# The first routing's clearings and its lists, and the places of VectorE's side work in two mixture networks, moved on one Trainium2 core

## The chip, the cores and the metric

The kernel runs on one core of one Trainium2 chip. The metric is device microseconds (us) of one execution, the median of three runs. A core has four compute engines with instruction queues of their own, TensorE (PE; its weight loads are shown apart, as PEld), VectorE (DVE), ScalarE (ACT) and GpSimd (POOL); each works through its queue in order and waits where an operand isn't there. SyncE (SP) issues most of the DMA transfers, also in order.

## The reference

```python
x = np.fft.fft(np.fft.fft(x, axis=1), axis=2).real      # 8 x 3072 x 256, then 24576 rows of 256
# first network (moe): 8 experts, dense
logits = x @ w_gate; P = np.exp(logits - logits.max())
for _ in range(8):
    P /= P.sum(1, keepdims=True) + 1e-09
    P /= P.sum(0, keepdims=True) + 1e-09
    P *= N / E
out = sum(P[:, e:e+1] * (np.maximum(x @ w1[e], 0) @ w2[e]) for e in range(8))
# second network (moe2): each row goes to its best expert
probs = softmax(out @ w_gate2); e = argmax(probs)
out2[row] = probs[row, e] * (np.maximum(out[row] @ u1[e], 0) @ u2[e])
```

Each expert is 256 to 1024 to 256 wide. P is the exponential of the logits less the largest of *all* rows, so most rows have weights that are zero in float32, and their output is zero. The kernel lists the rows that are left and computes those alone; a dense version stands behind a flag, for inputs where the lists don't hold.

## The kernel before

**The stages.** Fourier transform (to about 200 us); *first routing* (`route1`, to about 240 us), which makes the lists of rows and gathers the rows; first network (`moe1`, to about 430 us); *second routing* (`route2`, to about 448 us); second network (`moe2`, to the end).

**The lists.** The first routing gives every row that is left a place in one of 29 tiles of 128 rows, three for each of eight experts and five "free" tiles for the rest. A row's place is turned into a list by matmuls: VectorE compares a row of place numbers with all 128 (`ah`, in `rows`), which gives one matrix of zeros and ones per column of the row store, and TensorE multiplies each with a mask of 58 columns (`pt<-bv,ah` in `runs`, L572). The 64 columns are cut into chunks by `CH1`, now (24, 24, 16). From the product come the row numbers (`j`, `li`, `hr`, `pp`, `Rhidx`), then the signs (`Rsg`) and, in `signs()`, the places of the rows that are shared (`eq`, `gq`, `bq`) with 24 more thin matmuls (`late`, `bq`). Into this the caller puts other work by hooks: the string table `G2` says what each hook does. "g" is one half of the gate products of an expert's second layer (`gates2`, L1279, sixteen matmuls in two letters), "l" the store of the logits, "z" six clearings and the clearings of `acc`, "v" two matmuls on zeros, and a digit a part of expert 0's weights.

**Clearings.** The output is mostly zero. `zeros(2)` sends 512 KB from the zero tile `zt` to `out_dram`, as one transfer on SP's queue; SP also carries the weight loads (`rawa`, `rawb`, `rawc`) and the store of `Gd`, the gate weights that the free experts read.

**Gathers and builds.** `grab(j)` gathers the three tiles of group j with three indirect DMAs on GpSimd (`Xg<-H,Rhidx`, L818). The spectrum is stored by halves, so a row of x is put together from the two parts of a gathered row: VectorE adds two pairs of edge columns (33 and 32), multiplies the second half by the sign, copies two columns, and adds and subtracts 127 (the lists of functions a, b, c, d in the build, L1622 and L1641). For group 0 this runs tile by tile ahead of the first network; for the others the table `BUILD` says in which slots.

**A network.** For each expert three tiles together: `turn` transposes x (L869), `first` does eight products of six matmuls (L916), each into one of four buffers `ph`, and ScalarE and VectorE read each buffer into `hh` and `hl` (L438); `second` (L949) multiplies by the second weights, tile by tile, into `py`. Weights are split in a high part, on ScalarE, and a low part (`w1l`, `w2l`, L852), on VectorE. Experts 1 to 5 are followed by a "free" tile with the weights of any expert (`free`, "spill" experts).

**Slots.** VectorE's side work is placed by hand. A `Slots` table runs what was put at (expert, slot): slots 0 to 7 stand behind the eight products of `first`, 8 to 10 in the free tile, 11 behind the turn, 12 to 20 three to each tile of `second`. `BUILD`, `LOGIT` (first logits), `STEPS` (the Sinkhorn turns), `PROB` (the second network's probabilities) and the closing lists (`later`, nine operations each, returned by `positions`) are placed so.

```python
        h = moe.first(W[s, e], xt, lambda m: sl.run(e, m))
        if 0 <= f < n and e + 1 < E:
            flat()
        if e + 1 < E and f >= 0:
            xt = moe.turn(xs(e + 1))
        sl.run(e, 11)
```

Of the kernel before, what the change touches and what calls it, by code (L numbers as in the profile page):

```python
# [7 lines left out]
F32 = mybir.dt.float32  # L8
F32R = mybir.dt.float32r
BF16 = mybir.dt.bfloat16  # L10
# [360 lines left out]
CH1, CH2 = (24, 24, 16), (10, 10, 9)  # L371
# [75 lines left out]
class Route:  # L447
# [9 lines left out]
    def positions(self, T, M, n, rst, nf_, hook=lambda: None, S=None, n1=None, between=()):  # L457
# [56 lines left out]
        def later():  # L514
# [5 lines left out]
            s1, s2 = R["sel"][:, :nf_], S([nf_, 8], name="s2_")  # L520
# [54 lines left out]
def route1(nc, rt, L, rmx, K, R, keep, pool, ring, hooks):  # L575
# [4 lines left out]
    S = lambda sh, dt=F32, name=None: keep.tile([128] + list(sh), dt, name=name)  # L580

# [77 lines left out]
    gp, later = rt.positions(T, M, NSA, C("rst"), NF1, during, S, NSL)  # L659
# [35 lines left out]
    def signs():  # L695

        o.cp(lst, pv)
# [3 lines left out]
        o.ts(R["valid"], lst[:, 0], 0.5, ALU.is_ge)  # L701
        o.ts(sf, lst[:, 1], 127.5, ALU.is_ge)
        o.stt(R["prim"], sf, -1.0, R["valid"], ALU.mult, ALU.add)
        o.stt(R["ow"], R["hidx"], 2.0, sb, ALU.mult, ALU.add)

        o.tt(eq, ja[:, NSL:NSL + 8, None].to_broadcast([128, 8, NSL]), ja[:, None, :NSL].to_broadcast([128, 8, NSL]), ALU.is_equal)
        o.tt(eq, eq, gp[:, None, :NSL].to_broadcast([128, 8, NSL]), ALU.mult)
        o.red(gq, eq, ALU.add)
        tq, rq, _ = rt.split(T, gq, None, 8, "q")
# [41 lines left out]
def route2(nc, rt, lg, K, R, pool, ring, arrive, more, counts, warm):  # L751
# [3 lines left out]
    T = lambda sh, dt=F32, name=None: pool.tile([128] + list(sh), dt, name=name)  # L755
    mx, km, rk, kp = T([NT1], name="mx"), T([NT1], name="km"), T([NT1, 8], name="rk"), T([NT1], name="kp")
# [1139 lines left out]
```

## Time and profile before

| what | value |
|---|---|
| median of 3 runs | 639.26 us (638.91 to 639.56) |
| the profiled execution's own time | 638.99 us |
| its span in the profile | 637.2 us |
| TensorE (PE) | 615.2 us busy, 97% of the span, 4778 instructions |
| VectorE (DVE) | 435.4 us, 68% |
| ScalarE (ACT) | 328.6 us, 52% |
| GpSimd (POOL) | 194.1 us, 30% |

The page of the profile gives each engine's busy time, then the span in 40 equal slices of 15.9 us: each digit is the busy share in tenths (9 is 90% or more), and the line PEclk is TensorE's granted clock in tenths of full speed. The trace behind it answers closer questions: the busy time of each engine in chosen windows, what an engine waited for, and a timeline of single instructions with the idle time before each and what ended it. A matmul's weight load runs beside the matmul ahead of it.

### The profile page before, as it was taken

How to read it: one execution, taken by the hardware profiler on the slowest of the kernel's cores; microseconds unless marked ns; L12 is line 12 of the kernel's file. 1: busy time of each engine (PE TensorE's matmuls, PEld its weight loads, DVE VectorE, ACT ScalarE, POOL GpSimd, SP SyncE). 2: the span in 40 equal slices, each digit the busy share in tenths (PEclk: the TensorE clock that was granted, in tenths of full speed). 3: DMA queues.
4: the chain of work that ended last, by engine and by line, in shares of the span. 5: the costliest groups of instructions: out<-in, count | busy, mean ns of one | idle time of the engine just before them, and what ended most of it. 6: DMA issues, size and time to landing. Idle time of an engine off the chain costs nothing. (4 is left out here: it accounts for less than half of the span.)

```text
span 637.2 us, 12627 instructions
## 1 busy us (share of the span) xinstructions
PE 615.2 (97%) x4778; PEld 593.4 (93%) x4783; DVE 435.4 (68%) x981; ACT 328.6 (52%) x756; POOL 194.1 (30%) x318
## 2 busy tenths in 40 slices
PE   9999999999999999999999999999999999999995
PEld 6889999999999998999899999986899999999995
DVE  3697877688346977759898796856755664754760
ACT  3455555555544504547566468642455564654551
POOL 0002201221011058871201101223785655422422
PEclk9999999999999958999999999999999999999998
DMA  8999999999998976787877989863655548436421
GB/s 211 284 247 273 275 274 285 279 264 296 341 338 246 414 274 223 221 304 258 281 238 289 338 299 239 196 179 61 224 181 190 197 160 308 184 137 275 175 83 38
DMA packets 56927, 152.56 MB, mean 239 GB/s; under 512 B 8307, under 2 KB 25851, under 8 KB 49436
## 3 DMA queue, kind: packets, MB, share of 16 engines
q1 hardware_dynamic: 47644, 114.69, 58.2%
q0 software_dynamic: 8752, 36.50, 16.8%
q8 instruction: 39, 0.64, 0.4%
q10 hardware_dynamic: 464, 0.51, 0.2%
q14 instruction: 28, 0.23, 0.1%
HBM read 101.50 MB, written 50.07 MB: 238 GB/s over the span
## 5 line engine op out<-in xcount | busy, mean ns | idle before, releaser
L438 DVE SCALAR_TENSOR_TENSOR hl<-ph,hh 128x384 fp32r<-128x384 f32 (+1 forms) x161 | 85.1, 543 | 78.0 <-ACT hh L902 77.8
L949 PE MATMUL py<-w2h,hh 128*128 128x256 f32 (+1 forms) x472 | 136.0, 288 | 0.9 <-ACT lg L1678 0.9
L949 PE MATMUL py<-w2h,hl 128*128 128x256 f32 (+1 forms) x472 | 133.7, 283 | 1.1 <-DVE hl L438 1.0
L949 PE MATMUL py<-w2l,hh 128*128 128x256 f32 (+1 forms) x472 | 133.1, 282 | 0.3 <-DVE w2l L854 0.3
L902 ACT ACTIVATE hh<-ph 128x384 fp32r<-128x384 f32 (+1 forms) x161 | 75.9, 481 | 57.4 <-PE ph L916 33.9
L949 PEld LDWEIGHTS py<-w2h,hl 128*128 128x128 f32 x472 | 88.8, 188 | 1.9 <-DVE hl L438 1.9
L949 PEld LDWEIGHTS py<-w2h,hh 128*128 128x128 f32 x472 | 88.9, 188 | 1.5 <-ACT lg L1678 1.3
L949 PEld LDWEIGHTS py<-w2l,hh 128*128 128x128 f32 x472 | 89.1, 189 | 0.5 <-DVE w2l L854 0.5
L916 PE MATMUL ph<-xh,w1h 128*128 128x384 f32 x256 | 68.2, 347 | 4.0 <-DVE hl L438 3.2
L916 PE MATMUL ph<-xh,w1l 128*128 128x384 f32 x256 | 65.8, 339 | 0.0
L916 PE MATMUL ph<-xl,w1h 128*128 128x384 f32 x256 | 65.6, 338 | 0.0
L823 POOL DMA_INDIRECT out_dram<-y,Rorow x30 | 34.8, 1159 | 86.4 <-ACT hh L902 43.7
L126 POOL TENSOR_TENSOR lc<-hd 128x32 f32<-128x32 f32 x23 | 9.0, 393 | 164.5 <-ACT hd L122 150.5
L74 PE MATMUL pp<-ca,w 96*128 96x96 f32 x512 | 59.0, 275 | 0.0
L74 PEld LDWEIGHTS pp<-ca,w 96*128 96x128 f32 x512 | 58.2, 192 | 0.5 <-ACT Z L97 0.2
L916 PEld LDWEIGHTS ph<-xh,w1h 128*128 128x128 f32 x256 | 45.4, 190 | 6.6 <-DVE hl L438 4.8
L84 DVE COPY t<-pp 128x512 f32<-128x512 f32 (+2 forms) x56 | 33.3, 609 | 23.9 <-PE pp L82 23.9
L91 PE MATMUL pp<-cb,t 128*128 128x128 f32 x368 | 47.5, 276 | 0.6 <-DVE t L84 0.6
L916 PEld LDWEIGHTS ph<-xh,w1l 128*128 128x128 f32 x256 | 46.9, 190 | 0.0
L76 ACT ACTIVATE at<-pp 128x384 f32<-128x384 f32 x64 | 31.0, 490 | 30.6 <-PE pp L74 30.1
L916 PEld LDWEIGHTS ph<-xl,w1h 128*128 128x128 f32 x256 | 46.7, 190 | 0.0
L91 PEld LDWEIGHTS pp<-cb,t 128*128 128x128 f32 x368 | 44.4, 192 | 0.9 <-DVE t L84 0.8
(346 smaller groups left out, 1251.0 us busy)
## 6 DMA issues: line engine op xcount, KB each, us to landing
out_dram<-zt SPq DMA_DIRECT2D x48, 512.0 KB, 7.2
H<-hd SPq DMA_DIRECT2D x24, 562.0 KB, 10.2
xa<-in_xa_dram SPq DMA_DIRECT2D x32, 384.0 KB, 11.1
xm<-in_xm_dram SPq DMA_DIRECT2D x32, 384.0 KB, 8.7
rawa<-in_w_dram SPq DMA_DIRECT2D x8, 1024.0 KB, 8.2
rawb<-in_w_dram SPq DMA_DIRECT2D x8, 1024.0 KB, 5.1
rawa<-in_u_dram SPq DMA_DIRECT2D x8, 1024.0 KB, 8.9
rawb<-in_u_dram SPq DMA_DIRECT2D x8, 1024.0 KB
```

The costliest lines, as they stand in the source:

```text
L74: nc.tensor.matmul(p[:M, i], lhs(4 * h + i), ca, start=True, stop=True)
L76: nc.scalar.activation(out=at[:M, :, :, s0:s0 + 4], in_=p[:M].rearrange("m s g j -> m g j s"), func=AF.Copy)
L84: nc.vector.tensor_copy(out=t[:, :n, :M], in_=p[:, :n, :M])
L91: nc.tensor.matmul(p[:M, i * 128:(i + 1) * 128], t[:, i, :M], cb[:, (g0 + i) * 128:(g0 + i + 1) * 128], start=True, stop=True)
L126: eng.tensor_tensor(out=lc[:np_, :n], in0=hd[:np_, :, 129:137], in1=hd[:np_, :, 273:281], op=ALU.add)
L438: self.nc.vector.scalar_tensor_tensor(out, a, s, b, op0, op1)
L823: nc.gpsimd.indirect_dma_start(out=dst, out_offset=bass.IndirectOffsetOnAxis(ap=idx, axis=0), in_=src, in_offset=None, **kw)
L902: self.nc.scalar.activation(out=a[:, :n], in_=p[:, :n], func=AF.Relu)
L916: self.nc.tensor.matmul(p[:, :N], w, xx, start=(i == 0), stop=(i == 5))
L949: self.nc.tensor.matmul(p[:, :nd], c, W[2 + m // 4][w][:, m % 4, :nd], start=(m == 0 and i == 0), stop=(m == 7 and i == 2))
```

## The change

In the first routing:

- `CH1` becomes (24, 16, 16, 8), and hook 5 puts four matmuls on zeros ("vv") between the first chunk's 24 thin matmuls and the second's.
- Of the six clearings ahead of the gathers one stays ("a"); five are issued after the first three gathers, and they wait for a GpSimd memset of eight columns of `zt` that stands behind those gathers.
- On VectorE `eq` (two operations) goes ahead of `j`; the first `w1l` of expert 0 goes from ahead of `j` to behind `signs()`; `Rvalid`, `sf` and `Rprim` go to expert 0's slot 2 (`kinds`); `Rng`, the negated sign, is new.
- The build of group 0 loses the multiply by the sign: two fused operations (multiply, then add) take the place of the add and the subtract.
- The nine closing list operations go from expert 0's slot 4 to slot 18; their inputs lie in the pool that is kept.

In the networks:

- `BUILD`, `LOGIT` and `STEPS` are changed: group 1's last two functions go from slot 6 to 11 and 12 of expert 0, group 7's build from expert 5's second stage to expert 6's first; two Sinkhorn turns move by a slot.
- The second `w2l` of each of the first network's five free experts goes to slot 2 of its expert.
- Second network: the low parts `behind` go from slot 0 of expert 0 to slot 1, the part u3 from 1 to 3, two probabilities from (0, 4) to (0, 3) and from (0, 1) to (0, 5), the nine closing operations of the second routing from ahead of the network to (0, 12), the first free expert's weights, on GpSimd, from ahead of the gathers to (0, 14).

```diff
-CH1, CH2 = (24, 24, 16), (10, 10, 9)
+CH1, CH2 = (24, 16, 16, 8), (10, 10, 9)
...
-    gp, later = rt.positions(T, M, NSA, C("rst"), NF1, during, S, NSL)
+    gp, later = rt.positions(T, M, NSA, C("rst"), NF1, during, Q, NSL)
...
     for n in CH1:
         ah = rt.rows(ring, rb, a, n)
-        if late is None:
+        first = late is None
+        if first:
             late = ah
             spans(0, GL, "p")
             hooks[3]()
         rt.runs(pl, ah, bv, a, n, a == NSL, a + n == NSL)
+        if first:
+            hooks[4]()
         a = (a + n) % NSA
-    hooks[4]()
     eq, gq = T([8, NSL], name="eq"), T([8], name="gq")
+    o.tt(eq, ja[:, NSL:NSL + 8, None].to_broadcast([128, 8, NSL]), ja[:, None, :NSL].to_broadcast([128, 8, NSL]), ALU.is_equal)
+    o.tt(eq, eq, gp[:, None, :NSL].to_broadcast([128, 8, NSL]), ALU.mult)
...
+    def kinds():
+
+        o.ts(R["valid"], lst[:, 0], 0.5, ALU.is_ge)
+        o.ts(sf, lst[:, 1], 127.5, ALU.is_ge)
+        o.stt(R["prim"], sf, -1.0, R["valid"], ALU.mult, ALU.add)
+
     def targets():
 
+        kinds()
...
-                            elif c == "z":
-                                for _ in range(6):
-                                    zeros(2)
+                            elif c == "a":
+                                zeros(2)
...
-                signs, later = route1(nc, rt, L, rmx, K, R, S, r1, ring, [fill(i) for i in range(1, 5)] + [lambda: low(0, 1)])
+                signs, later = route1(nc, rt, L, rmx, K, R, S, kp, r1, ring, [fill(i) for i in range(1, 6)])
...
-                for j in (0, 1):
-                    grab(j)
-                fill(5)()
+                grab(0)
+
+                nc.gpsimd.memset(zt[:, 0, 0:8], 0.0)
+                for _ in range(5):
+                    zeros(2)
+                grab(1)
+                fill(6)()
                 signs()
-                fill(6)()
+                low(0, 1)
+                fill(7)()
...
-BUILD = ((0, (5, 6, 6, 6)), (1, (0, 1, 2, 3)), (2, (1, 2, 3, 4)), (2, (12, 13, 14, 16)), (3, (12, 13, 14, 16)), (5, (0, 1, 2, 3)), (5, (12, 13, 14, 16)))
+BUILD = ((0, (6, 6, 11, 12)), (1, (0, 0, 1, 2)), (2, (1, 2, 4, 5)), (2, (12, 13, 14, 16)), (3, (12, 13, 14, 16)), (5, (0, 1, 2, 3)), (6, (1, 1, 2, 4)))
...
-LOGIT = ((0, 11), (0, 11), (0, 13), (0, 20), (1, 5), (1, 12), (1, 18), (2, 2), (0, 16), (2, 7))
+LOGIT = ((0, 11), (0, 11), (0, 13), (0, 20), (1, 4), (1, 12), (1, 18), (2, 2), (0, 16), (2, 7))
...
-STEPS = [3, 4, 10, 10, 17, 17, 23, 24, 32, 32, 39, 39, 48, 48, 55, 55, 62, 63]
+STEPS = [3, 4, 11, 11, 17, 17, 23, 24, 32, 32, 39, 39, 48, 48, 54, 54, 62, 63]
...
-PROB = ((0, 4, 0), (0, 1, 1), (1, 11, 8), (2, 6, 2), (3, 4, 3), (4, 4, 4), (4, 11, 9), (5, 4, 5), (6, 4, 6), (7, 5, 7))
+PROB = ((0, 3, 0), (0, 5, 1), (1, 11, 8), (2, 6, 2), (3, 4, 3), (4, 4, 4), (4, 11, 9), (5, 4, 5), (6, 4, 6), (7, 5, 7))
...
-G2 = ("g", "", "ggggggg", "0lg1zg2g3", "gg", "gg", "g")
+G2 = ("g", "", "ggggggg", "0lg1ag2g3", "gg", "vv", "gg", "g")
...
         if 0 <= f < n:
+            behind = [] if s == "w" else None
+            if s == "w":
+                sl.at(e, 2, lambda b=behind: b.pop()())
             for i in (4, 5):
-                sl.at(e + at[i] // 21, at[i] % 21, lambda f=f, i=i, g=g: free.part(f, i - 2, g(i)))
+                sl.at(e + at[i] // 21, at[i] % 21, lambda f=f, i=i, g=g, b=behind if i == 5 else None: free.part(f, i - 2, g(i), b))
...
             if i is not None:
-                v = X[j][:, t, 137:264]
-                tt(v, v, R["sg"][:, CAP * j + i:CAP * j + i + 1, None].to_broadcast([128, 1, 127]), ALU.mult)
                 return
...
+        def pair(g, c):
+            o.stt(x[j][:, i, c], X[j][:, i, 137:264], g[:, CAP * j + i:CAP * j + i + 1], X[j][:, i, 2:129], ALU.mult, ALU.add)
...
-    for i, f in zip((0, 1, 2, 3, 4), (lambda: rest[3](1, 1), rest[0], lambda: rest[3](1), rest[1], begin)):
+    for i, f in zip((0, 1, 2, 3, 4, 18), (lambda: rest[3](1, 1), rest[0], lambda: rest[3](1), rest[1], begin, rest[5])):
         sl.at(0, i, f)
...
-    sl.at(0, 0, *behind)
-    sl.at(0, 1, lambda: part("u", 0, 3, V))
-    free.weights(0)
+    sl.at(0, 1, *behind)
+    sl.at(0, 3, lambda: part("u", 0, 3, V))
+    sl.at(0, 12, later)
+    sl.at(0, 14, lambda: free.weights(0))
```

**VectorE, first routing, from the last chunks of `ah` to the build of the first tile.** Before:

```order
L429 TENSOR_TENSOR ah<-irx,rba 128x3072
L429 TENSOR_TENSOR ah<-irx,rba 128x2048
L852 TENSOR_TENSOR w1l<-rawa,w1h 128x1024
L435 TENSOR_SCALAR j<-pt 128x29
...
L441 COPY lst<-pt 128x58
...
L429 TENSOR_TENSOR eq<-ja 128x320
L429 TENSOR_TENSOR eq<-eq,gsa 128x320
L444 TENSOR_REDUCE gq<-eq 128x8
...
L1622 TENSOR_TENSOR Xg<-Xg 128x32
L1622 TENSOR_TENSOR Xg<-Xg,Rsg 128x127
L1641 COPY x<-Xg 128x2
L1622 TENSOR_TENSOR x<-Xg 128x127 x2
```

And with the change:

```order
L429 TENSOR_TENSOR ah<-irx,rba 128x2048 x2
L429 TENSOR_TENSOR ah<-irx,rba 128x1024
L429 TENSOR_TENSOR eq<-ja 128x320
L429 TENSOR_TENSOR eq<-eq,gsa 128x320
L435 TENSOR_SCALAR j<-pt 128x29
...
L438 SCALAR_TENSOR_TENSOR Row<-Rhidx,sb 128x29
L860 TENSOR_TENSOR w1l<-rawa,w1h 128x1024
L1635 TENSOR_TENSOR Xg<-Xg 128x33
L1635 TENSOR_TENSOR Xg<-Xg 128x32
L1653 COPY x<-Xg 128x2
L438 SCALAR_TENSOR_TENSOR x<-Xg,Rsg 128x127
L438 SCALAR_TENSOR_TENSOR x<-Xg,Rng 128x127
```

`w1l` now stands behind the lists instead of ahead of them, `eq` the other way round, and each tile's build has five operations instead of six.

**SP and GpSimd, around the first gathers.** SP before:

```order
L1340 DMA Ld<-L 128x1552
L1210 DMA out_dram<-zt 128x2x512 x6
L1348 DMA acc<-zt 128x512 x3
L1348 DMA acc<-zt 128x54
L1292 DMA Gd<-g_76 128x8x64
L1233 DMA rawa<-in_w_dram 128x2048
```

SP with the change:

```order
L1348 DMA Ld<-L 128x1552
L1218 DMA out_dram<-zt 128x2x512
L1355 DMA acc<-zt 128x512 x3
L1355 DMA acc<-zt 128x54
L1218 DMA out_dram<-zt 128x2x512 x5
L1300 DMA Gd<-g_76 128x8x64
L1241 DMA rawa<-in_w_dram 128x2048
```

GpSimd with the change (before, the first row has six gathers and the memset of `zt` isn't there):

```order
L826 DMA Xg<-H,Rhidx 128x281 x3
L1387 MEMSET zt 128x8
L826 DMA Xg<-H,Rhidx 128x281 x3
L1382 MEMSET grow 8x256 x2
L826 DMA Xg<-H,Rhidx 128x281
```

Five clearings now stand behind the clearings of `acc`, ahead of the store of `Gd` and of the load of expert 1's weights, and GpSimd has the memset between its first two groups of gathers.

**VectorE, the start of the first expert with a free tile.** Before:

```order
L852 TENSOR_TENSOR w2l<-rawc,w2h 128x4x256
L854 TENSOR_TENSOR w2l<-gd,w2h 128x4x8
L1622 TENSOR_TENSOR x<-Xg 128x3x127
L852 TENSOR_TENSOR w2l<-rawc,w2h 128x4x256
L854 TENSOR_TENSOR w2l<-gd,w2h 128x4x8
...
L444 TENSOR_REDUCE cs<-P 128x8
L438 SCALAR_TENSOR_TENSOR hl<-ph,hh 128x384 x2
L438 SCALAR_TENSOR_TENSOR hl<-ph,hh 128x256
L438 SCALAR_TENSOR_TENSOR hl<-ph,hh 128x384 x2
```

And with the change:

```order
L444 TENSOR_REDUCE cs<-P 128x8
L438 SCALAR_TENSOR_TENSOR hl<-ph,hh 128x384 x2
L438 SCALAR_TENSOR_TENSOR hl<-ph,hh 128x256
L438 SCALAR_TENSOR_TENSOR hl<-ph,hh 128x384 x2
L1635 TENSOR_TENSOR Xg<-Xg 128x2x33
L1635 TENSOR_TENSOR Xg<-Xg 128x2x32
L438 SCALAR_TENSOR_TENSOR hl<-ph,hh 128x384
L860 TENSOR_TENSOR w2l<-rawc,w2h 128x4x256
L862 TENSOR_TENSOR w2l<-gd,w2h 128x4x8
L438 SCALAR_TENSOR_TENSOR hl<-ph,hh 128x384
```

A `w2l` that stood ahead of the expert's `hl` (those with 384 columns; the one with 256 is a free tile's) now stands between them, behind the third of slot 2.

## Rows read from the trace of the kernel before

**Rows 1.** The page, shares of the engines and the clock line.

```profile
PE 615.2 (97%) x4778; PEld 593.4 (93%) x4783; DVE 435.4 (68%) x981; ACT 328.6 (52%) x756; POOL 194.1 (30%) x318
...
PEclk9999999999999958999999999999999999999998
```

**Rows 2.** Windows (us): PE, PEld, DVE, ACT, POOL busy; PE clock; DMA share; GB/s.

```profile
224.00:225.00 1.00, 0.72 (x11) 0.73 (x11) 1.00 (x2) 0.00 (x0) 0.00 (x0) 0.50 1.06 412
...
244.00:245.00 1.00, 1.00 (x6) 1.00 (x6) 1.00 (x2) 0.07 (x1) 1.00 (x2) 0.79 0.92 366
```

**Rows 3.** TensorE's waits, 240 to 432 us: sum us, times, longest.

```profile
PE ph L916 <- DVE hl L438: 2.4, 4, 1.0
...
PE py L949 <- DVE hl L438: 1.0, 2, 0.8
```

**Rows 4.** Timeline, 218 to 229 us: start, duration, instructions [idle before <- releaser].

```profile
219.09 1.95 PE L1279 MATMUL py<-wg,rawc 128*128 128x96 f32 x16
...
222.47 2.89 DVE L429 TENSOR_TENSOR ah<-irx,rba 128x3072 bf16<-128x3072 bf16 x2
...
224.28 2.88 PE L572 MATMUL pt<-bv,ah 128*128 128x58 bf16 x40 [1.29 <-DVE ah L429]
...
228.83 0.49 DVE L429 TENSOR_TENSOR eq<-ja 128x320 f32<-128x320 bf16 x1
```

**Rows 5.** Timeline, 226 to 246 us.

```profile
226.98 3.71 PE L1279 MATMUL py<-wg,rawc 128*128 128x96 f32 x16
...
228.21 1.12 POOL L818 DMA_INDIRECT Xg<-H,Rhidx  x1 [32.77 <-DMA out_dram<-zt]
...
234.20 0.30 DVE L1622 TENSOR_TENSOR Xg<-Xg 128x33 f32<-128x33 f32 x2 [1.54 <-DMA Xg<-H,Rhidx]
234.41 0.28 DVE L1622 TENSOR_TENSOR Xg<-Xg,Rsg 128x127 f32<-128x127 f32 x1
...
237.01 1.22 DVE L852 TENSOR_TENSOR w1l<-rawa,w1h 128x1024 fp32r<-128x1024 f32 x1
...
239.05 1.49 PE L869 MATMUL pt<-ident,x 128*128 128x128 f32 x6
...
240.91 1.07 PE L916 MATMUL ph<-xh,w1h 128*128 128x384 f32 x2 [0.37 <-ACT xh L872]
...
244.74 0.51 PE L916 MATMUL ph<-xh,w1h 128*128 128x384 f32 x2
...
245.78 0.51 PE L916 MATMUL ph<-xh,w1h 128*128 128x384 f32 x2
```

**Rows 6.** Timeline, 435 to 449 us, the second routing's end.

```profile
436.16 3.20 PE L1298 MATMUL py<-zb 128*128 128x512 bf16 x13
...
442.06 1.02 POOL L818 DMA_INDIRECT Xg<-acc,Rgidx  x1 [5.85 <-DVE Rgidx L429]
...
445.07 0.43 PE L869 MATMUL pt<-ident,Xg 128*128 128x128 f32 x2 [0.50 <-DMA Xg<-acc,Rgidx]
...
447.48 0.44 PE L869 MATMUL pt<-ident,Xg 128*128 128x128 f32 x2
...
448.39 0.83 PE L916 MATMUL ph<-xh,w1h 128*128 128x384 f32 x2 [0.47 <-ACT xh L872]
```

**Rows 7.** Timeline, 311 to 316 us, an expert with a free tile.

```profile
311.33 1.22 DVE L852 TENSOR_TENSOR w2l<-rawc,w2h 128x1024 fp32r<-128x1024 f32 x1
...
313.18 0.61 PE L916 MATMUL ph<-xh,w1h 128*128 128x384 f32 x2 [1.00 <-DVE hl L438]
```

**Rows 8.** Timeline, 451 to 456 us, the second network's first stage.

```profile
455.87 0.44 PE L916 MATMUL ph<-xh,w1h 128*128 128x384 f32 x1 [0.75 <-DVE hl L438]
```

**Rows 9.** GpSimd's timeline, 261 to 283 us.

```profile
271.89 1.36 POOL L818 DMA_INDIRECT Xg<-H,Rhidx  x1 [0.16 <-issue]
```

**Rows 10.** The tile Xg, 225 to 285 us.

```profile
DMA to landing us min/median/max: 2.9/4.3/7.2
```

**Rows 11.** VectorE's timeline, 279 to 281 us.

```profile
279.88 0.17 DVE L429 TENSOR_TENSOR sg__3039<-Xg 128x24 f32<-128x24 f32 x1
```

More of the change, by code (lines that the diff above doesn't have):

```diff
@@ L580, in route1 @@
     S = lambda sh, dt=F32, name=None: keep.tile([128] + list(sh), dt, name=name)
+    Q = lambda sh, dt=F32, name=None: stay.tile([128] + list(sh), dt, name=name)
     m1 = S([1], name="m1")
@@ L695, in signs @@
     def signs():
-        o.cp(lst, pv)
         sb = T([NT1], I32, name="sb")
@@ L700, in signs @@
         o.ts(R["sg"], sb, -2.0, ALU.mult, 1.0, ALU.add)
[L701 to L707, printed above, removed]
         o.red(gq, eq, ALU.add)
+        o.ts(R["ng"], sb[:, :CAP], 2.0, ALU.mult, -1.0, ALU.add)
+        o.cp(lst, pv)
         tq, rq, _ = rt.split(T, gq, None, 8, "q")
@@ L721, in signs @@
         rt.more()
+        o.stt(R["ow"], R["hidx"], 2.0, sb, ALU.mult, ALU.add)
         pq = rt.py.tile([128, 512], F32, name="py")
@@ L748, in route1, with route2 @@
     return signs, (targets, overflow, later)
-def route2(nc, rt, lg, K, R, pool, ring, arrive, more, counts, warm):
+def route2(nc, rt, lg, K, R, stay, pool, ring, arrive, more, counts, warm):
     o = rt.o
@@ L755, in route2 @@
     T = lambda sh, dt=F32, name=None: pool.tile([128] + list(sh), dt, name=name)
+    S = lambda sh, dt=F32, name=None: stay.tile([128] + list(sh), dt, name=name)
     mx, km, rk, kp = T([NT1], name="mx"), T([NT1], name="km"), T([NT1, 8], name="rk"), T([NT1], name="kp")
@@ L790, in route2 @@
     more(counts[2])
-    gp, later = rt.positions(T, M, NT1, C("rst2"), NF2, during, between=at)
+    gp, later = rt.positions(T, M, NT1, C("rst2"), NF2, during, S, between=at)
     tb, rb, _ = rt.split(T, gp, (cs, ca), NT1, "b", tp)
@@ L1317, in run @@
                 r1a = P(s1, "r1a", 3, side="right")
-                ring = lambda n: r1a.tile([128, n], BF16, name="ah")
+                ring = lambda n: (r1a if n == 128 * max(CH1) else r1).tile([128, n], BF16, name="ah")
                 late.update({"1": w1p, "2": w2p})
@@ L1390, in rest @@
                 def rest():
-                    later[2]()
                     sp.close()
@@ L1400, in ask @@
                     zeros(2)
-                turned, more = moe1(nc, K, R, rt, lg, hot, acc, moe, W, part, X, xg, Gd, *rows("w1", "w2"), xb, pt, zeros, zt, later[:2] + (rest, low, grab), ask, rt.C("tro"), lambda i: None, lambda: xg.tile([128, CAP, HW], F32, name="Xg").rearrange("p a b -> p (a b)")[:8, :512])
+                turned, more = moe1(nc, K, R, rt, lg, hot, acc, moe, W, part, X, xg, Gd, *rows("w1", "w2"), xb, pt, zeros, zt, later[:2] + (rest, low, grab, later[2]), ask, rt.C("tro"), lambda i: None, lambda: xg.tile([128, CAP, HW], F32, name="Xg").rearrange("p a b -> p (a b)")[:8, :512])
             with ExitStack() as s1:
@@ L1430, in arrive @@
                     choose(0, NT1)
-                later = route2(nc, rt, lg, K, R, r2, ring, arrive, more, Y2, lambda: warm(W3))
+                later = route2(nc, rt, lg, K, R, kp, r2, ring, arrive, more, Y2, lambda: warm(W3))
                 def grab2(j):
@@ L1449, in run @@
                 xt = moe.turn(lambda i: X[0][:, i], lambda i: warm(3) if i < CAP - 1 else None)
-                later()
             fm, fi = kp.tile([128, 1], F32, name="fm"), kp.tile([128, 1], I32, name="fi")
@@ L1462, in run @@
                 yb = P(s1, "yb2", 4)
-                moe2(nc, R, out, moe, W, part, X, xg, *rows("u1", "u2"), yb, check, grab2, xt, behind)
+                moe2(nc, R, out, moe, W, part, X, xg, *rows("u1", "u2"), yb, check, grab2, xt, behind, later)
     flag = nc.values_load(fi[0:1, 0:1], min_val=0, max_val=1)
@@ L1598, in weights, with part @@
             self.w[f, i] = t
-    def part(self, f, i, eng):
+    def part(self, f, i, eng, later=None):
         g = self.w[f, 2][:, 4 * (i - 2):4 * (i - 1)] if self.Gd is not None else None
-        self.w2.setdefault(f, {})[i] = self.moe.part(self.w[f, 1][:, i % 2], i, eng, g)
+        self.w2.setdefault(f, {})[i] = self.moe.part(self.w[f, 1][:, i % 2], i, eng, g, later)
     def turn(self, q, xs, n):
@@ L1800, in moe1, with moe2 @@
     return q, more
-def moe2(nc, R, out, moe, W, part, X, xg, w1f, w2f, yb, check, grab, xt, behind):
+def moe2(nc, R, out, moe, W, part, X, xg, w1f, w2f, yb, check, grab, xt, behind, later):
     o = Ops(nc)
```

17 lines of the change are left out of this document (11 added, 6 removed).

## The prediction

> **What bounds the kernel now.** I read the page's shares and clock line first, then one-microsecond windows, TensorE's waits, and the timelines of the places that these point to. TensorE is busy for 615.2 of 637.2 us, and its clock line is full except in two of the forty slices, from about 223 to 255 us [rows 1]. So there is little else than TensorE, and two things to win from it: some 22 us in which it waits, and the time that it spends at half clock. The windows place the second: from 224 us the granted clock is 0.50 (1.2 GHz), and only in the window from 244 to 245 does it come back to full (2.4 GHz) [rows 2]. That is 20 us in the first routing and the start of the first network. The waits between 240 and 432 us are small: 2.4 us in four places for a product buffer that VectorE's `hl` frees late, and 1.0 us in two for `hl` itself [rows 3].
>
> The timeline shows what came before the fall. TensorE had 24 thin matmuls (58 columns) of the first list chunk, then waited 1.29 us for VectorE's next `ah`, then had 40 more [rows 4]. The price of the fall is seen on one form: sixteen matmuls of the gate products take 1.95 us at 219.09 and 3.71 us at 226.98 [rows 4, 5]. From 226.98 to 239.05 TensorE doesn't wait once, and the turn of the first tile group follows on at once [rows 5]. So what sets the first network's start today is not the gather and not VectorE but TensorE's own queue at 1.2 GHz. The first stage (L916) starts at 240.91, and its third group at 244.74: 3.83 us for two groups, where one takes 1.04 us from there on [rows 5].
>
> **The change part by part.** *The hole in the lists.* The second chunk shrinks from 24 to 16 columns' worth. Its comparison takes 2048/5120 of 2.89 us, 1.16 us, so it is there at 222.47 + 1.16 = 223.63 [rows 4]. Four filler matmuls of 512 columns stand in the gap; thirteen of this form took 3.20 us, or 0.25 us each [rows 6]. TensorE, free at 224.28 - 1.29 = 222.99, is busy with them to 223.97 and then finds `ah` ready. The other 40 thin matmuls (2.88 us) end at 226.85, 0.31 us sooner than now. That the clock stays at 1.00 through this is the choice on which the forecast rests. For it: the only stretch without work is filled with dense matmuls, and the gate products that stand ahead of the hole held 1.00 as they are. Against it: 40 thin matmuls still follow, and no row shows how thin a stretch may be.
>
> *From the list to the first stage, at full clock.* TensorE's part: the two gate batches take about 1.95 us each, to 230.8; the 24 thin matmuls of `bq` (24 of the 40 in 2.88 us: 1.7 us) [rows 4] wait for VectorE until about 231; a third batch of 1.95 us ends at 234.8. VectorE's part: it was done with the lists at 234.20 - 1.54 = 232.66, 4.45 us after the first gather was issued [rows 5]. The first gather now goes out at 228.21 - 0.31 = 227.90. Two `eq` of 0.49 us, 1.05 us with their gaps [rows 4], move ahead of the list, under the last thin matmuls; three operations on 29 columns move into the network and `Rng` on 3 comes in (0.4 us out and 0.1 us in, estimates from operations on 33 columns in 0.30 us a pair); one `w1l` of 1.22 us, which lay in the old gap, comes in too [rows 5]. So VectorE reaches the build at 227.90 + 4.45 - 1.05 - 0.4 + 1.3 = 232.2. Three tiles took 237.01 - 234.20 = 2.81 us; without the multiply each is 0.2 us shorter (an estimate from the add of the same 127 columns in 0.28 us, gap included), 2.2 us in all [rows 5], if a fused operation costs no more than the add it replaces: built at 234.4. The last transposes led to the first stage in 448.39 - 447.48 = 0.91 us in the second routing, at full clock [rows 6]. TensorE being free at 234.8, the first stage starts at about 235.6, not 240.91: 5.3 us. Its first two groups take 2.1 us and not 3.83, 1.75 us more; the second `w1l` (1.22 us) now ends after the start and holds `xl` up, 0.5 us back. **Term A: 6.5 us**; bounds 0.3 (the clock falls all the same, only the shorter list is left) and 7.0 (`xl` is not late).
>
> *The gathers and the clearings.* Five of six 512 KB clearings leave the time ahead of the gathers, where the DMA engines are full [rows 2], and wait on SP for a GpSimd memset of `zt` that stands behind three gathers. Today VectorE waits 1.54 us for the first tile, which lands 234.20 - 228.21 = 5.99 us after its issue [rows 5]; in the second routing it is 445.07 - 442.06 = 3.01 us [rows 6]. I take 3.01: 230.9, ahead of VectorE's 232.2, so nothing is charged beyond A. Behind the clearings on SP stand the store of `Gd` and expert 1's loads. The store needs the last gate batch (234.8) and the next load the second `w1l` (about 235.7), so I charge nothing; if that cover fails, ScalarE's `w1h` for expert 1 is late in slot 7 of expert 0.
> The Trainium skill (DMA: Bandwidth & Descriptors, section Queues, rings and completion order) says that each DMA engine serves the queues it has work for in turn, a packet at a time. By that rule clearings would slow a gather and not stand ahead of it, and moving them buys less than my two rows say; the second rival below has the time for that.
>
> *Expert 0.* Nine list operations leave slot 4 for slot 18, and two halves of the second build leave slot 6 for 11 and 12, where no `hl` is due. TensorE's two waits there are 1.0 us [rows 3]. **Term B: 0.8 us** of it, since three operations (`Rvalid` to `Rprim`) come in.
>
> *Low parts of the spill networks.* Five times the second `w2l` moves to slot 2 of its expert. At 311.33 it stood before four `hl` and cost TensorE 1.00 us at 313.18 [rows 7]; all four such waits are 2.4 us [rows 3]. Behind three `hl` it is 1.23 us of delay against four product buffers of 1.04 us each. **Term C: 1.5 us**, bounds 0 and 2.4. The other builds and Sinkhorn turns move by a slot or into a later expert; I cost them at nothing, as they stay beside work of TensorE in the same queue, and put what they may give into the range.
>
> *Second network's start.* The nine list operations and the first probabilities no longer stand between VectorE and its first `hl`; the one wait is 0.75 us at 455.87 [rows 8]. **Term E: 0.7 us.** The first spill expert's weights move behind nine gathers on GpSimd; they serve expert 2, some 40 us on.
>
> *New waits.* GpSimd's gathers are paced by GpSimd, so they don't come sooner. The third of tile group 6 is issued at 271.89 [rows 9] and lands a median of 4.3 us later [rows 10], at 276.2. Its logits run at 279.88 [rows 11]; 7.3 us sooner (A and B) they are due at 272.6, so VectorE will stand for 3.6 us, late in expert 1's second stage, when it owes TensorE nothing at once. **Term F: -0.9 us**, between 0 and 3.6.
>
> The sum: 6.5 + 0.8 + 1.5 + 0.7 - 0.9 = 8.6 us off the profiled execution's own 638.99 us, 630.4. That execution lies 0.27 us under the median of the three runs (639.26), so I forecast 630.7.
>
> **The rivals.** First, *the clock falls all the same*: the change doesn't do what it says. Then the gate batches take 3.71 us again and A is 0.3. B, C and E stay and F goes, as nothing is sooner: 638.99 - 0.3 - 3.0 + 0.27 = 636.0. For it speaks the thinness of what follows the fillers, against it that the gap is gone. Second, *the clearings were not what held the gather*: it lands after 5.99 us again, at 233.9, and three builds end at 236.1 and not 234.4: 1.7 us later, 632.4. That is also the time by the page's rule. For it speaks that the moved clearings still overlap the later gathers, against it the 3.01 us. Third, on the other side, *VectorE's in-order queue becomes what the first stages wait for*: five low parts of 1.23 us in slot 2, and the stand of 3.6 us, are paid by TensorE in full, 9.8 us, and C is lost. Against A, B and E (8.0 us) that is 638.99 + 1.8 + 0.27 = 641.1. It decides where VectorE's delay in one first stage passes what the product buffers hold, about 4 us; for it speaks the 1.00 us at 313.18 behind a delay of 1.23, against it that three `hl` now run first.
>
> **How the numbers follow.** Forecast 0.62, first rival 0.22, second 0.07, third 0.06, others 0.03. A measurement of this kernel tells 0.2%, 1.28 us, from no change. Faster by more: forecast and second rival, and most of the first (which needs 1.3 of its 3.3 us), 0.84. Within: the tail of the first, 0.08. Slower: the third and others, 0.08. The low end takes A at 7.0, B at 1.0, C at 2.4, E whole, F at zero, and 0.6 for the moved builds: 627.5. The high end is the first rival with half of its gain, 637.5.
>
> **What would show it.** A: the clock line stays full after 223 us; no wait for `ah`; the first stage near 235.6; sixteen gate matmuls in 1.95 us behind the list. The clearings: the first tile some 3 us after its issue. B and C: no waits for `hl` in expert 0 and at the fourth group of the spill experts; F: VectorE waiting for `Xg` near 273 us. E: no wait near 446 us. Wrong: a clock at 0.50 behind the list (first rival), an L916 wait for `hl` growing beyond 2.4 us (third).

## The result: 634.67 us, and the profile after

The changed kernel took 634.67 us (median of 14 runs, 628.28 to 641.14), the kernel before beside it 639.41 us (14 runs, 635.75 to 645.39); the ratio is 0.9906 (95% interval 0.9883 to 0.9929), about 6 us less; the two medians differ by 4.7 us. A ratio leaves out slow runs, those over 1.5% above the fastest of their kernel (four of the change's fourteen here, four of e8's twelve below), and a median doesn't. On two further chips the same kernel gave 0.994 (0.9918 to 0.9963) and 0.9948 (0.9927 to 0.9969), 3.9 and 2.5 us by the medians (e1 and e12 below). So 2.5 to 6 us is what can be said of the change's worth. The forecast was 630.7 us, range 627.5 to 637.5: faster, as said, but less than the 8.6 us of the sum.

The profiled execution alone looks better than that. It took 628.28 us, the fastest of the 14. Its page, which answers to [rows 1]:

```profile
PE 608.1 (97%) x4781; PEld 586.6 (94%) x4787; DVE 433.8 (69%) x980; ACT 329.4 (53%) x756; POOL 194.0 (31%) x319
...
PEclk9999999999999999999999999999999999999998
```

The clock line is full up to the last slice. The timeline of the lists in the changed kernel, to be held against [rows 4, 5]:

```profile
219.75 1.87 PE L572 MATMUL pt<-bv,ah 128*128 128x58 bf16 x24
...
221.68 0.81 PE L1359 MATMUL ph<-zb 128*128 128x512 bf16 x3
...
222.36 2.83 PE L572 MATMUL pt<-bv,ah 128*128 128x58 bf16 x40
...
225.03 2.00 PE L1287 MATMUL py<-wg,rawc 128*128 128x96 f32 x16
...
226.25 1.12 POOL L826 DMA_INDIRECT Xg<-H,Rhidx  x1 [32.17 <-DVE sb L433]
...
228.93 0.95 POOL L826 DMA_INDIRECT Xg<-H,Rhidx  x1 [0.30 <-issue]
...
230.32 0.29 DVE L1635 TENSOR_TENSOR Xg<-Xg 128x33 f32<-128x33 f32 x2
...
232.61 0.30 DVE L1635 TENSOR_TENSOR Xg<-Xg 128x33 f32<-128x33 f32 x2 [0.49 <-DMA Xg<-H,Rhidx]
...
233.35 0.59 PE L877 MATMUL pt<-ident,x 128*128 128x128 f32 x2 [0.61 <-DVE x L438]
...
234.25 0.82 PE L924 MATMUL ph<-xh,w1h 128*128 128x384 f32 x2 [0.32 <-ACT xh L880]
...
236.99 0.51 PE L924 MATMUL ph<-xh,w1h 128*128 128x384 f32 x2
```

The matmuls on zeros fill the hole, sixteen gate matmuls take 2.00 us and not 3.71, and VectorE finds the first tile there: it landed at most 4.07 us after its issue (226.25 to 230.32). The last wait is new: the third tile, gathered at 228.93, is there 3.7 us later, and TensorE waits 0.61 us for its build.

TensorE's waits for VectorE's `hl` and for the build, from 200 us to the end (they all lie at the end of the lists and in the first network), to be held against [rows 3]:

```profile
PE ph L924 <- DVE hl L438: 2.6, 2, 2.0
PE pt L877 <- DVE x L438: 0.6, 1, 0.6
```

The two waits for `hl` in expert 0 (1.0 us) are gone. Of the four at the free experts (2.4 us) one of 0.6 us is left, and one of 2.0 us is new. In the timeline the new one is what the prediction called term F:

```profile
269.94 0.95 POOL L826 DMA_INDIRECT Xg<-H,Rhidx  x1 [0.16 <-issue]
...
277.95 0.18 DVE L429 TENSOR_TENSOR sg__3034<-Xg 128x24 f32<-128x24 f32 x1 [7.19 <-DMA Xg<-H,Rhidx]
...
278.97 0.62 PE L924 MATMUL ph<-xh,w1h 128*128 128x384 f32 x2 [1.96 <-DVE hl L438]
...
304.38 0.62 PE L924 MATMUL ph<-xh,w1h 128*128 128x384 f32 x2 [0.62 <-DVE hl L438]
```

VectorE stands 7.2 us for the third gather of tile group 6, and four `hl` are queued behind it. Group 6 is the eighth that is gathered (the order is 0, 1, 2, 8, 3, 4, 5, 6), so this is the 24th gather. It goes out at 269.94, sooner than in the kernel before (271.89 [rows 9]), but takes longer to land. The tile `Xg` in a window that holds this issue alone, with the change (269.5 to 271 us) and before (271.8 to 273.5):

```profile
  DVE sg__3034 L429: 7.2, 1
...
DMA to landing us min/median/max: 7.9/7.9/7.9
```

```profile
DMA to landing us min/median/max: 6.0/6.0/6.0
```

Where the stages begin splits the time. Two starts are not in the rows above. The first thin matmul of the kernel before:

```profile
221.14 1.84 PE L572 MATMUL pt<-bv,ah 128*128 128x58 bf16 x24
```

and the second routing's first matmuls on zeros and the second network's first product in the changed kernel:

```profile
425.82 3.20 PE L1306 MATMUL py<-zb 128*128 128x512 bf16 x13
...
438.10 0.82 PE L924 MATMUL ph<-xh,w1h 128*128 128x384 f32 x2 [0.47 <-ACT xh L880]
```

All profiles of this study, read in the same way (us; to the first thin matmul, from there to the first network's first product, to the second routing's first zeros, to the second network's first product, to the end of the span):

| profile | chip | Fourier | lists | first network | second routing | second network | span |
|---|---|---|---|---|---|---|---|
| before | A | 221.1 | 19.8 | 195.3 | 12.2 | 188.8 | 637.2 |
| change | A | 219.8 | 14.5 | 191.6 | 12.3 | 188.4 | 626.5 |
| e1, change | B | 224.1 | 14.9 | 191.7 | 12.3 | 188.9 | 631.9 |
| e2, no zeros | B | 222.0 | 16.3 | 192.0 | 12.3 | 188.2 | 630.8 |
| e3, lists only | B | 224.3 | 17.4 | 195.5 | 12.2 | 188.0 | 637.3 |
| e4, clearings first | B | 223.7 | 15.5 | 191.7 | 12.3 | 187.6 | 630.7 |
| e5, before | C | 222.5 | 17.4 | 196.0 | 12.3 | 188.5 | 636.7 |
| e6, low parts back | C | 223.7 | 17.5 | 192.6 | 12.2 | 188.4 | 634.4 |
| e7, lists back | C | 222.5 | 18.9 | 193.2 | 12.3 | 189.0 | 635.8 |
| e8, one memset | C | 224.3 | 21.5 | 197.4 | 12.3 | 189.6 | 645.0 |
| e9, clearings late | D | 221.7 | 18.8 | 190.9 | 14.3 | 187.7 | 633.3 |
| e10, logits later | D | 222.0 | 18.8 | 192.8 | 12.4 | 188.5 | 634.6 |
| e11, both | D | 221.8 | 18.8 | 192.4 | 15.9 | 187.9 | 636.7 |
| e12, change | D | 221.9 | 18.9 | 190.9 | 12.2 | 189.4 | 633.2 |

On chip A 1.4 of the 10.7 us between the two profiles lie in the Fourier transform, which the change doesn't touch; 5.3 lie in the lists, 3.7 in the first network, 0.4 in the second. The first network takes 190.9 to 191.7 us in the three profiles of the change and 195.3 and 196.0 us in the two of the kernel before. The lists' stage has no such order: 14.5, 14.9 and 18.9 us with the change, 19.8 and 17.4 before.

### The profile page after: what moved, and what is told of

Same layout as the page of the kernel before. It is cut to its first block, busy times and chain, and to the rows that moved or that the text cites. A ratio compares the mean times of both kernels' runs of the same rounds, so it can differ in the third digit from the quotient of the medians.

```text
span 626.5 us, 12648 instructions
## 1 busy us (share of the span) xinstructions
PE 608.1 (97%) x4781; PEld 586.6 (94%) x4787; DVE 433.8 (69%) x980; ACT 329.4 (53%) x756; POOL 194.0 (31%) x319
```

## The experiments

**e1, the change again.** No edit.

> The changed kernel once more, nothing edited. Its profiled execution kept the clock at 1.00 and took 628.3 us, while the median of its executions was 634.7 us, with mean granted clocks of 0.982 to 0.997. Theory 1: in the other executions the clock still falls in the first routing's lists, only sometimes and for less long than before. Then a profile with a mean clock near 0.99 shows some 8 to 12 us at 0.50 between 220 and 240 us, and the instructions elsewhere lie as in the first profile. Rival: the half-clock time lies elsewhere (Fourier transform, second routing, second network), and the lists are cured. Then that profile shows 1.00 from 220 to 240 us and the fall in another place. Median expected at 633 to 636 us by both.

Measured: 633.92 us against 637.8 us before, ratio 0.994 (0.9918 to 0.9963). The lists' stage held the clock and took 14.9 us. The half-clock time lies in the Fourier transform, near 17 and near 48 us, and that stage is 4.4 us longer than on chip A. The rival holds for this profile: the lists are cured, and what is lost is elsewhere.

**e2, without the matmuls on zeros.**

```diff
-G2 = ("g", "", "ggggggg", "0lg1ag2g3", "gg", "vv", "gg", "g")
+G2 = ("g", "", "ggggggg", "0lg1ag2g3", "gg", "", "gg", "g")
```

> The changed kernel without the four matmuls on zeros in the lists; the smaller second chunk stays, so TensorE stands there for about 0.7 us instead of 1.3. Theory 1 (the hole is what the clock falls on): it falls in every execution behind the hole, sixteen gate matmuls take 3.7 us again, the first network starts some 5 us later, and the mean clock is near 0.98: 635 to 637 us. Rival (a shorter hole is enough, the matmuls on zeros do nothing): times and clocks as with them, 633 to 636 us, and 628 where the clock holds.

Measured: 634.74 us, 0.9962 (0.9936 to 0.9988). The clock fell behind the hole, as theory 1 said; two rows of its timeline:

```profile
224.60 2.84 PE L572 MATMUL pt<-bv,ah 128*128 128x58 bf16 x40 [0.75 <-DVE ah L429]
...
227.26 3.71 PE L1287 MATMUL py<-wg,rawc 128*128 128x96 f32 x16
```

But the stage is only 1.4 us longer than e1's, and the kernel 0.8 us, which the intervals don't tell apart. The fall lasted 6.8 us, not 20.5, and part of it lay beside the wait for the gathered tiles (1.0 us in e1, none here).

**e3, the lists' part alone.** The kernel before with `CH1` of 24, 16, 16, 8 and the hook with "vv".

```diff
-CH1, CH2 = (24, 24, 16), (10, 10, 9)
+CH1, CH2 = (24, 16, 16, 8), (10, 10, 9)
...
-G2 = ("g", "", "ggggggg", "0lg1zg2g3", "gg", "gg", "g")
+G2 = ("g", "", "ggggggg", "0lg1zg2g3", "gg", "vv", "gg", "g")
```

> The kernel before with the chunks of 24, 16, 16 and 8 and the four matmuls on zeros alone; clearings, builds, low parts and closing lists stay as they were. Theory (most of the gain is the clock in the lists): TensorE no longer waits, but the six clearings still lie ahead of the gathers, so the first gather lands some 6 us after its issue and the first network starts about 2 us later than in the change: 3 to 5 us off the kernel before when the clock holds, with the networks as before. Rival (the gather behind the clearings sets the start): TensorE waits at the first transpose for VectorE, the clock falls there, and the gain is under 1.5 us.

Measured: 639.3 us, 1.0016 (0.9992 to 1.0039): nothing. The first hole is filled, and the next one takes its place:

```profile
234.60 1.82 PE L572 MATMUL py<-bq,ah 128*128 128x16 bf16 x24 [1.26 <-DVE bq L429]
```

VectorE still does `w1l` and `eq` within the lists, `bq` is late, and the clock is at half for 10 us behind this wait. So the zeros alone are worth nothing. That VectorE's new order is what they lack is read from this wait; the order wasn't added by itself (the clearings and the shorter build are missing here too).

**e4, all clearings ahead of the gathers.**

```diff
                             elif c == "a":
-                                zeros(2)
+                                for _ in range(6):
+                                    zeros(2)
...
-                nc.gpsimd.memset(zt[:, 0, 0:8], 0.0)
-                for _ in range(5):
-                    zeros(2)
```

> The changed kernel with all six clearings ahead of the first gathers again, without the memset of the zero tile. Theory (clearings hold the first gather): the first tile lands 5 to 6 us after its gather's issue instead of 4.1 at most, TensorE waits for the tiles at the first transposes, and the first network starts 1.5 to 2.5 us later than in the change at the same clock; if the clock falls in that wait, it is 5 us or more. Rival (gathers and clearings share the DMA engines, so the order does not matter): the landing stays at about 4 us, and the start and the time stay within 0.5 us of the change at the same clock.

Measured: 633.49 us, 0.9933 (0.9909 to 0.9957), no worse than e1 on the same chip. The gather was held, by at least 1.5 us (5.59 us from issue to use instead of at most 4.07):

```profile
230.22 1.12 POOL L826 DMA_INDIRECT Xg<-H,Rhidx  x1 [32.16 <-DMA out_dram<-zt]
...
235.81 0.30 DVE L1633 TENSOR_TENSOR Xg<-Xg 128x33 f32<-128x33 f32 x2 [1.42 <-DMA Xg<-H,Rhidx]
```

The stage is 0.6 us longer than e1's all the same: where the first tile comes at once, the third tile ends the stage, since GpSimd issues it 2.7 us later. Moving the clearings bought nothing that can be measured.

**e5, the kernel before again.** No edit.

> The kernel before, nothing edited, for a second profile. The first profile of it held the clock at 1.00 in the Fourier transform and fell only in the lists (19.8 us from the lists' first matmul to the first network); three of four profiles of kernels with the change's lists, or a part of them, fall near 17 and near 48 us in the Fourier transform, which makes that stage 2 to 4.5 us longer. Theory 1 (that fall belongs to the execution, not to the kernel): it is here too, the lists' stage takes 15 to 20 us and the first network 195.3. Rival (the change brings it, though it touches nothing there): the Fourier transform holds 1.00 and ends near 221 us.

Measured: 638.45 us, a single run. Theory 1 holds: the kernel before falls near 48 us too, so that fall isn't the change's. And the fall in the lists is another one. Two rows of its timeline, then windows (columns as in [rows 2]):

```profile
225.65 2.88 PE L572 MATMUL pt<-bv,ah 128*128 128x58 bf16 x40 [1.28 <-DVE ah L429]
...
228.35 3.71 PE L1279 MATMUL py<-wg,rawc 128*128 128x96 f32 x16
```

```profile
226.00:228.00 2.00, 2.00 (x33) 2.00 (x33) 1.86 (x2) 0.00 (x0) 0.00 (x0) 0.62 1.05 407
228.00:230.00 2.00, 2.00 (x17) 2.00 (x16) 1.33 (x10) 0.00 (x0) 0.41 (x1) 0.50 1.05 408
230.00:232.00 2.00, 2.00 (x11) 2.00 (x11) 1.89 (x6) 0.00 (x0) 1.70 (x2) 0.50 1.07 398
232.00:234.00 2.00, 2.00 (x14) 2.00 (x14) 1.79 (x15) 0.20 (x1) 1.39 (x3) 0.67 0.69 228
```

The same wait (1.28 us, 1.29 in [rows 4]) is followed by 6.8 us at half clock (twice the missing clock in each window: 1.5, 2, 2 and 1.3), where the first profile has 20 us. The lists' stage is 17.4 us, not 19.8.

**e6, the free experts' low parts at their old place.**

```diff
-            behind = [] if s == "w" else None
-            if s == "w":
-                sl.at(e, 2, lambda b=behind: b.pop()())
+            behind = None
```

> The changed kernel with the second low part of each of the five free experts back at its old place, ahead of its expert's first products. By the prediction's term C the first network is 1.5 us longer than the change's 191.6 us (bounds 0 and 2.4), with waits of about 1 us for the product buffer at the fourth group of the experts with a free tile. Rival (the other moves made the first network shorter): it stays within 0.3 us of 191.6.

Measured: 637.27 us against 640.37 us before on this chip, 0.9957 (0.9929 to 0.9985). The first network took 192.6 us, 1.7 more than e12's 190.9, the profile it is most like (both start the network at half clock), though on another chip. One wait at the fourth group is longer:

```profile
311.49 0.61 PE L924 MATMUL ph<-xh,w1h 128*128 128x384 f32 x2 [1.84 <-DVE hl L438]
```

It is 0.62 us there in e12 (and in the change), and behind the longer wait the clock was at half for another 3.4 us. All waits for `hl` in the first network are 2.5 us, 1.5 more than e12's. Term C fits, as far as one profile on each side can show it.

**e7, the closing lists and the second group's build at their old places.**

```diff
-    for i, f in zip((0, 1, 2, 3, 4, 18), (lambda: rest[3](1, 1), rest[0], lambda: rest[3](1), rest[1], begin, rest[5])):
+    for i, f in zip((0, 1, 2, 3, 4, 4), (lambda: rest[3](1, 1), rest[0], lambda: rest[3](1), rest[1], rest[5], begin)):
...
-BUILD = ((0, (6, 6, 11, 12)), (1, (0, 0, 1, 2)), (2, (1, 2, 4, 5)), (2, (12, 13, 14, 16)), (3, (12, 13, 14, 16)), (5, (0, 1, 2, 3)), (6, (1, 1, 2, 4)))
+BUILD = ((0, (5, 6, 6, 6)), (1, (0, 0, 1, 2)), (2, (1, 2, 4, 5)), (2, (12, 13, 14, 16)), (3, (12, 13, 14, 16)), (5, (0, 1, 2, 3)), (6, (1, 1, 2, 4)))
```

> The changed kernel with the nine closing list operations back in slot 4 of expert 0 and the second group's build back in slots 5 and 6. By term B the first network is 0.8 us longer (191.6 to 192.4 us), with waits for the low half of the hidden rows at the start of expert 0's second stage, 1.0 us in all. Rival (they were hidden, and the clock's return alone took those waits away): within 0.2 us of 191.6.

Measured: 639.68 us, 0.998 (0.9953 to 1.0007). The first network took 193.2 us, 2.3 more than e12's (again on another chip), and TensorE's waits show where 1.7 of them are:

```profile
PE py L957 <- DVE hl L438: 1.7, 3, 0.8
```

e12 has no such row. By this pair term B was too small.

**e8, gathers closer together.**

```diff
-                            for _ in range(2):
+                            for _ in range(1):
                                 nc.gpsimd.memset(grow, 0.0)
```

> The changed kernel with one memset of eight rows between two gathers of the first routing instead of two; no result depends on it. In the change VectorE stands 7.2 us for the third gather of tile group 6, issued at 273.5 us, and TensorE 2.0 us for VectorE. Theory (term F: the gathers' pace on GpSimd sets this wait): each gather comes 0.33 us sooner than the one before it, eleven of them 3.6 us by then, VectorE's stand falls to about 3.6 us and TensorE's 2.0 us go: the first network takes 189.6 us, and the whole 2 us less than the change. Rival (gathers that come faster collide with the weight loads on the DMA engines): they land later after their issue, a low or high part of a weight is late, and nothing is won.

Measured: 644.6 us against 640.37 us before, 1.0015 (0.9979 to 1.0052); the profile's lists' stage is 21.5 us and its first network 197.4. Neither theory said how: the gathers follow each other in 1.42 us instead of 1.77, and the engines stand for nothing that the profile shows ("issue", and "remote" where the releaser is outside the trace):

```profile
243.73 0.20 ACT L1289 ACTIVATE g<-py 128x32 f32<-128x32 f32 x1 [9.99 <-remote]
...
245.70 1.02 DVE L429 TENSOR_TENSOR xl<-pt,xh 128x384 fp32r<-128x384 f32 x2 [6.41 <-issue]
...
245.72 1.07 PE L924 MATMUL ph<-xh,w1h 128*128 128x384 f32 x2 [6.15 <-issue]
```

VectorE's stand for group 6 is gone, but the network starts so late here that this doesn't test term F (e12, below, has a late start and little of the stand too). The expectation also took the wrong gather: the one issued at 273.5 us is two later than the one that VectorE waits for.

**e9 to e12, one chip.** e9 takes the five clearings out of the first routing; e10 does two groups' logits later; e11 does both; e12 is the change.

```diff
-                nc.gpsimd.memset(zt[:, 0, 0:8], 0.0)
-                for _ in range(5):
-                    zeros(2)
...
-ZERO = [(), (16, 19), (9, 11, 13, 15, 17, 19), (9, 11, 13, 15, 17, 19), (9, 11, 13, 15, 17, 19), (2, 5), (2,), ()]
+ZERO = [(), (16, 19), (9, 11, 13, 15, 17, 19), (9, 11, 13, 15, 17, 19), (9, 11, 13, 15, 17, 19), (2, 5, 13, 16, 19), (2, 13, 16), ()]
```

> The changed kernel with the five clearings behind the first gathers taken out there (and the memset with them) and sent in experts 5 and 6 instead. In two profiles of the change the lists' stage (first thin matmul to first network) took 14.5 and 14.9 us; in three profiles of kernels with the change's lists on another chip it took 17.5, 18.9 and 21.5 us, with ScalarE standing 6.6 to 10 us ahead of its third gate copy, and TensorE and VectorE standing for nothing that the profile shows, all while the DMA engines were full. Theory (those clearings make the DMA engines full just then, and that is what the engines stand for): without them the lists' stage is 14 to 15 us, these stands are under 1 us, and the time is 1 to 3 us less than the change's on the same chip, if experts 5 and 6 have room. Rival (the weight loads and gathers fill the engines anyway): the stage stays as long as the change's on this chip and nothing is won.

```diff
-LOGIT = ((0, 11), (0, 11), (0, 13), (0, 20), (1, 4), (1, 12), (1, 18), (2, 2), (0, 16), (2, 7))
+LOGIT = ((0, 11), (0, 11), (0, 13), (0, 20), (1, 4), (1, 12), (2, 1), (2, 5), (0, 16), (2, 7))
```

> The changed kernel with the logits of tile group 6 from expert 1's slot 18 to expert 2's slot 1, and those of group 7 from expert 2's slot 2 to slot 5; no row is computed otherwise. Theory (term F: VectorE, in order, stands for a gather that is not needed yet): its stand of 7.2 us falls under 1 us, TensorE's 2.0 us for the product buffer go, and the first network takes 189.6 us instead of 191.6: 2 us off the change. Rival (VectorE has no room left in expert 2's first products): the waits come back there as several of about 1 us, and under 0.5 us is won.

> Both of the two edits: clearings late and the two logits later. If both theories hold, the gains add: lists' stage 14 to 15 us, first network 189.6 us, 3 to 5 us less than the change on the same chip. By the rivals: the time of the better of the two alone.

> The changed kernel, nothing edited, as what the three others are held against on this chip. Expected from the runs so far: 633 to 637 us; first network 191.6 us; the lists' stage 14.5 to 15 us if ScalarE does not stand, 17 to 19 us if it does.

Measured, against 639.41 us before: e9 641.64 (1.0029, 1.0005 to 1.0052), e10 638.57 (0.9969, 0.9943 to 0.9996), e11 640.64 (0.9996, 0.9965 to 1.0028), e12 636.93 (0.9948, 0.9927 to 0.9969). By the medians e9 and e11 are 4.7 and 3.7 us slower than the change; e10's 1.6 us are not told apart from nothing, since most of its interval lies within e12's.

On this chip the change's lists' stage is 18.9 us. ScalarE stands ahead of its third gate copy (7.9 us idle, 3.3 on chips A and B), and TensorE for it; then a window of e12 in which no engine but GpSimd works, and the same window of e9:

```profile
234.05 0.39 PE L1287 MATMUL py<-wg,w1l 128*128 128x96 f32 x2
...
240.03 0.20 ACT L1289 ACTIVATE g<-py 128x32 f32<-128x32 f32 x1 [7.94 <-remote]
...
240.74 1.07 PE L924 MATMUL ph<-xh,w1h 128*128 128x384 f32 x2 [3.34 <-ACT g L1289]
```

```profile
238.00:240.00 2.00, 0.00 (x0) 0.00 (x0) 0.00 (x0) 0.00 (x0) 1.78 (x4) 0.50 1.05 408
```

```profile
238.00:240.00 2.00, 0.00 (x0) 0.00 (x0) 0.00 (x0) 0.24 (x2) 1.77 (x4) 0.50 0.27 72
```

The copy's own matmuls end at 234.4 (234.05 + 0.39), and it runs at 240.03. In e9 the DMA engines are a quarter full then, and at most half full in the windows from 230 to 240 us, and ScalarE stands as long (7.9 us). So full DMA engines are not what it stands for: my theory falls. Nor does the stand belong to the change alone. In e5, the kernel before on chip C, the third copy's matmuls end at 237.99 and the copy runs 1.1 us later:

```profile
237.60 0.39 PE L1279 MATMUL py<-wg,w1l 128*128 128x96 f32 x2
...
239.11 0.20 ACT L1281 ACTIVATE g<-py 128x32 f32<-128x32 f32 x1 [4.37 <-PE pt L869]
```

And the late clearings cost in the second routing, where TensorE waits for the gathers:

```profile
442.20 0.43 PE L877 MATMUL pt<-ident,Xg 128*128 128x128 f32 x2 [2.46 <-DMA Xg<-acc,Rgidx]
```

It is 0.43 us in e12. The stage is 2.1 us longer; the rest of e9's loss isn't in its profile, which is that of the fastest of its thirteen runs. e11 has the same loss (15.9 us) and the clock at half there for 3.4 us. In e10 no 2.0 us came free, because e12 doesn't have them: the network starts 4 us later there, VectorE stands 1.2 us for group 6 instead of 7.2, and TensorE not at all. The first network is 1.9 us longer instead, without the rival's waits for `hl`: the clock stays at half for 10 us, where e12 has 7, which is worth most of it. Why it stays longer is open.

## Why the prediction was partly right

**Term A, 6.5 us,** was right for the execution that it was read from and wrong as a size for the kernel. On chip A's timeline the start was forecast for 235.6; taking off the 1.39 us by which the lists began sooner, that is 234.2, and 234.25 was measured. The first two groups took 2.74 us instead of 3.83. Together that is 6.4 us. But the step "That is 20 us in the first routing and the start of the first network" took one execution's fall for the kernel's. e5 has 6.8 us behind the same hole, and there the most that the lists' stage can give is 17.4 less 14.9: 2.5 us (an estimate across two chips). On chip C every profile with the change's lists has a stand of ScalarE and takes 17.5 to 21.5 us, where e5 takes 17.4: there the lists gave nothing. On chip D they take 18.8 and 18.9, with no profile of the kernel before beside them. What ScalarE stands for was not settled; not the clearings (e9), and closer gathers go with a longer stand (e8).

The mean granted clock, which is on record for every run on chips B to D, tells of the executions without a profile too. Twice the missing clock times the span is the time at half clock (an estimate, the mean over the runs): on chip B 19.4 us before, 13.5 with the change and 20.5 without the zeros; on chip D 20.6 before and 20.1 with the change. So the change holds the clock longer on chip B, and not on chip D. And time at half clock isn't time lost one for one: the 7 us between e1 and e2 cost 0.8 us, which the intervals don't tell from nothing.

**Its parts.** The zeros hold the clock (e2), but alone they are worth nothing (e3), and beside the rest their worth in time isn't shown. The clearings were worth nothing measurable: the landing was mis-read as what ends the stage, where the third tile's issue on GpSimd does (e4). The second rival had the effect right, that the move buys nothing, and the mechanism wrong, since the gather did come sooner. Its time was 0.4 us too long by the prediction's own sum: TensorE is free only at 234.8 there, so tiles built at 236.1 cost 1.3 us and not 1.7. e4 agrees with the rule that it was given beside (the Trainium skill, DMA: Bandwidth & Descriptors, section Queues, rings and completion order: queues are served in turn) so far as that the clearings slow a gather, by at least 1.5 us. Whether the gather took turns with them or stood behind them isn't shown: the DMA engines were still full from 232 to 234 us in e4 (a share of 1.02), and the tile was used at 235.81.

**Terms B and C** were 0.8 and 1.5 us. In chip A's two profiles the waits that went are 1.0 and 1.8 us (2.4 less the 0.6 that is left). e7 and e6, each held against one profile of another chip, give 2.3 and 1.7. Where B fell short, it counted the waits of one profile (1.0 us [rows 3]); e5 shows 1.7 us of them at the same place, e7 the same. On chip A the first network became 3.7 us shorter: 1.1 us are the clock in its first groups, 2.8 these waits, and F gave 2.0 back, which makes 1.9; with the sizes of e7 and e6 it is 3.1. The rest wasn't traced.

**Term F, -0.9 us,** had the place right and the size wrong: 2.0. It failed at the landing. The prediction gave the gather the median of all gathers from 225 to 285 us, 4.3 us, so that it would be there at 276.2; this gather took 6.0 us in the kernel before and 7.9 with the change, and was there at 277.8. VectorE also came for it sooner, at 270.76 (277.95 less 7.19) and not at 272.6. With the change SP issues a weight load and two clearings just ahead of this gather (267.98 and 268.37), which came behind it before (277.16 and 277.55); that they are what slows it wasn't tested. With the late start of chip D F is nothing.

**Term E, 0.7 us,** isn't shown in the stage: the second network takes 187.6 to 189.6 us in all profiles with the change's part and 188.0 to 188.8 in those without (before, e3, e5). The wait of 0.75 us that it counts is gone in the change's three profiles, and one of 0.2 to 0.4 us for ScalarE's `hh` is new.

**The rivals.** The first named the right time for chip D (636.0; measured 636.9), but not for its reason: the lists' matmuls held the clock in every profile with the zeros and VectorE's order, and where it fell it was in ScalarE's stand or right behind it. The third is refuted: it asked for 9.8 us, and the waits for `hl` were at most 2.8 us in the change's three profiles. They pass the 2.4 us that were named as its sign, but 2.0 and 2.2 us of them are F's one wait. That the range held is luck in part: it reached to the first rival, whose reason isn't what happened.

## What to carry to other kernels

A clock fall in one profile is a sample: before a whole forecast is put on its length, read the same place in a second execution. A hole in TensorE's queue is worth filling only together with the next one, and an engine that is freed early runs into whatever comes next on its chain (here the third gather's issue, then ScalarE). Moving VectorE's side work to slots where no product waits went with a shorter first network in every profile of the change. And when a wait for a transfer is forecast, the landing of that very transfer is worth reading, not the median of a window (6.0 us, not 4.3).

## What was not expected of the hardware

TensorE's clock fell in the Fourier transform between 45 and 56 us in all twelve later profiles, of both kernels, and in neither of the first two; that stage took 221.7 to 224.3 us there, 221.1 and 219.8 in the first two. On two of four chips ScalarE stood 6.6 to 10 us at one place of the change's lists (3.3 on the others), in six of the seven profiles with no releaser in the trace, whether the DMA engines were full (408 GB/s) or not (72 GB/s). And with gathers following each other on GpSimd in 1.42 us instead of 1.77 the kernel was no faster than the one before (1.0015), and that stand was the longest.
